# Attention followed by a feed-forward layer: the first 1427 scheduled operations follow a written list, the first loads change their order, and three early steps get more engines

## The chip, the cores and the metric

The kernel runs on one core of a Trainium2 chip. The time is the device time of one execution in microseconds; the kernel before has a median of 913.9 us over three runs (912.82 to 916.17). The engines of the core are TensorE (PE, with its weight loads as PEld), VectorE (DVE), ScalarE (ACT), GpSimd (POOL) and SyncE (SP), which here only issues DMAs. Each engine works through its own instructions strictly in the order in which the program was written.

## The reference

There are 8 batches, 8 heads, 576 positions and a head width of 64. Attention looks back over a window: heads 0 to 3 see the last 32 positions, heads 4 to 7 every fourth one of the last 128. The result goes through a feed-forward layer of 512 to 2048 to 512 whose activation is a quotient of two polynomials.

```python
scores = scale * np.matmul(q, k.transpose(0, 1, 3, 2))
scores = np.where(masks[None, :, :, :], scores, -1000000000.0)
attn = np.exp(scores - np.max(scores, axis=-1, keepdims=True))
attn = attn / (np.sum(attn, axis=-1, keepdims=True) + 1e-09)
x = np.matmul(attn, v)            # then [4608, 512]
h = x @ w_in
P = a[0] + a[1] * h + a[2] * h2 + a[3] * h3
Q = 1.0 + np.abs(b[0]) * np.abs(h) + np.abs(b[1]) * h2
return (P / (Q + 1e-06)) @ w_out
```

The weights arrive in 64-bit floats, so a 128x512 block of them is 512 KB.

## The kernel before

**Units.** Each batch's attention is cut into 6 units, 48 in all, numbered here as 0 to 47 (unit 6 is the first of batch 1). A unit loads its queries and keys (`load_qk`, 448 KB) and its values (`load_v`, 384 KB). `scores` is 48 small matmuls into a pair of PSUM banks; for batches 0 and 1 the mask is added by two or four matmuls before them. Then come `max` and `sub` on VectorE (units 6 to 11 subtract on TensorE, `sub_pe`; unit 4 does it within six exponentials, `exp_bank`), `exp` on ScalarE, `sum` and `recip` on VectorE, `norm` (GpSimd for batch 0, six ScalarE copies for batch 1), a transposition on TensorE (`transposes`, `place`) and `av`, 48 small matmuls with the values. For batch 0 the result is split from PSUM into a high and a low part (`evac_hi` on ScalarE, `evac_lo` on VectorE; `less_hi` and `copy_lo` for units 4 and 5). For later batches it goes out to DRAM and back in another layout (`put_out`, `move_out`: tiles `y` and `z` in the profile) and is split from there. From unit 8 on, the `av` of the unit two before runs together with the scores.

**Weights.** Each of the 32 weight blocks (`wi` and `wo`, 16 each) is loaded (`w_fetch`), made into 32-bit floats in three steps (`w_scale` on ScalarE, `w_low` on ScalarE or GpSimd, `w_join` on VectorE), and split into high and low (`w_hi` on ScalarE, VectorE or GpSimd; `w_lo` on VectorE or GpSimd).

**Tiles.** The feed-forward layer is 144 tiles, T0 to T143: 9 groups of 512 tokens by 16 blocks of the hidden width. A tile is `h` (12 matmuls of 128x512, high and low parts), an activation of twelve steps on ScalarE, VectorE and GpSimd, and four `out` of three matmuls each. T0 to T7 need batch 0's attention, T8 to T23 batch 1's. Two PSUM banks hold `h`; a bank comes free when the step `g2` (`a<-a,h` in the profile) has run. The steps named below: `q_lin` is `r<-a,ab_t` on ScalarE, `qq` is `a<-r,a` on VectorE or GpSimd, `g_hi` is `gh<-a`, `g_lo` is `gl<-a,gh`.

**The planner.** Every step is an operation (`op`) with the engines that may run it, its cost on each, and what it depends on. `Plan.run` goes through a modelled time, always takes the operation that can start first (with due times as ranks, lines 143 to 164), and emits its instructions; the emitted order is final on every engine. Where the model leaves TensorE idle in the first 150 us, `keep_busy` (line 217) emits filling matmuls of `ident_b`, whose result is not used. All loads are issued by SP in the emitted order, so a load that waits for a free buffer holds up the ones behind it. The early loads are put in the order of their ranks (lines 1029 to 1038).

**The start.** The masks and the six coefficients have loads of their own (`masked`, line 958, and `lc`, line 963), issued behind unit 0's queries and keys.

Of the kernel before, what the change touches and what calls it, by code (L numbers as in the profile page):

```python
# [25 lines left out]
BOTH = {"ACT": 480, "DVE": 520}  # L26
# [13 lines left out]

DEPTH, LOADS, STAGE, AHEAD, ON_PE, BY_PE = 2, 2, 6, 6, 2, 2
LEFT = S - 512
RQ, RKEY, NV = 4 * 3 * 32, 4 * 128, 3 * 2 * 2 * 64
# [18 lines left out]

class Op:
# [4 lines left out]
    def __init__(self, engs, rank, fn, deps, dma, lock):  # L68
        self.engs, self.rank, self.fn, self.dma, self.lock = engs, rank, fn, dma, lock
        self.deps = [d for d in deps if d is not None]  # L70
        self.takes, self.follows = [], []
        self.spare = None
# [9 lines left out]
class Plan:  # L82
# [7 lines left out]
    DMA_START, DMA_NS, DMA_RATE = 1000.0, 1700.0, 380.0  # L90
# [5 lines left out]
    def op(self, engs, rank, fn, *deps, dma=0, lock=False):  # L96
        o = Op(engs, rank, fn, deps, dma, lock)
        self.ops.append(o)
        return o
# [32 lines left out]
    def run(self):  # L132
        free = {}
        pipe, ports = self.DMA_START, 0.0
# [6 lines left out]
        ready = [o for o in self.ops if not left[id(o)]]  # L141
        done = 0
        while ready:
            options = []
            for o in ready:
                before = list(o.deps)
                for tag, _ in o.takes:
                    bufs, groups = self.tags[tag]
                    if len(groups) >= bufs:
                        users = groups[len(groups) - bufs]  # L150
                        if any(u.end is None for u in users):
                            break
                        before += users
                else:
                    for eng, ns in o.engs.items():
                        shared = ports if Plan.shares(o, eng) else 0.0
                        t = max([free.get(eng, 0.0), shared] + [d.after(eng) for d in before])
                        options.append((t, o, eng, ns))
            assert options, "the plan is stuck"
            first = min(x[0] for x in options)  # L160
            eng0 = min((x for x in options if x[0] == first), key=lambda x: x[1].rank)[2]
            start, o, eng, ns = min(
                (x for x in options if x[2] == eng0 and x[0] <= first + self.WINDOW), key=lambda x: (x[1].rank, x[0])
            )
            for tag, users in o.takes:
                self.tags[tag][1].append(users)
# [22 lines left out]
def tile_attention_moe(  # L189
# [27 lines left out]
    def keep_busy(n, ps):  # L217

        if n <= 0:
            return  # L220
# [881 lines left out]
```

## Time and profile before

| what | value |
|---|---|
| median of three runs | 913.9 us |
| profiled execution: span from first to last instruction | 911.9 us |
| PE, DVE, ACT, POOL busy | 887.7, 727.6, 684.8, 472.8 us |
| mean granted TensorE clock | 0.994 |
| T0's first matmul starts | 42.23 us |
| time of one `h`, and of one tile's four `out`, where nothing waits | 2.72 us each |

The profiled execution's own time is its span; the median of the runs is 2.0 us above it. A row of the stage table gives a stretch of the span, its length, then for each engine the busy time with the number of instructions, the granted TensorE clock, the DMA share and the rate. A row of a timeline gives start, duration, engine, line of the kernel, operation, tiles and in brackets the idle time before it with what ended it. L245, L248, L251, L254 and L257 are helper lines, so instructions are told apart by their tiles. In the groups, the number behind the busy time is the mean duration in ns.

### The profile page before, as it was taken

What the parts mean: (1) busy time and instruction counts of PE and PEld (TensorE: products, weight loads), DVE (VectorE), ACT (ScalarE), POOL (GpSimd) and SP (SyncE); (2) the same over time, 40 slices, a digit from 0 to 9 for tenths busy, and PEclk for the clock granted to TensorE, in tenths of its full rate; (3) what the DMA queues carried; (4) which work ended last, traced back from release to release, by engine and by line L of the source; (5) the groups of instructions that cost most, each with busy time, mean ns of one, the idle gap of its engine ahead of it and who ended that gap; (6) DMA issues with size and microseconds to landing.
All of it is one profiled execution on the core that took longest, in us unless ns stands there. A gap on an engine that the chain in (4) does not pass through costs nothing.

```text
span 911.9 us, 21320 instructions
## 1 busy us (share of the span) xinstructions
PE 887.7 (97%) x8208; PEld 714.9 (78%) x8208; DVE 727.6 (80%) x1291; ACT 684.8 (75%) x1128; POOL 472.8 (52%) x424
## 2 busy tenths in 40 slices
PE   6889999999999999999999999999999999999998
PEld 4656778877887888888888878888888888888876
DVE  4889999988998986888688886887688677566656
ACT  3888899867767777677767767777877788778774
POOL 2354666635555654555555555456455555544442
PEclk8899999999999999999999999999999999999999
DMA  9785614144643531453155441233143220001001
GB/s 339 272 281 181 241 55 147 60 127 143 192 141 113 152 93 46 131 165 112 49 173 156 135 141 65 96 104 98 47 145 108 63 70 1 0 1 47 1 1 46
DMA packets 85478, 103.46 MB, mean 113 GB/s; under 512 B 37377, under 2 KB 62849, under 8 KB 85377
## 3 DMA queue, kind: packets, MB, share of 16 engines
q1 hardware_dynamic: 85376, 102.11, 35.1%
q8 instruction: 64, 1.05, 0.5%
q14 instruction: 38, 0.30, 0.1%
HBM read 75.21 MB, written 26.87 MB: 112 GB/s over the span
## 4 chain that ended last, share of the span: by engine, by line
PE 82%; DVE 8%; DMA 4%; ACT 2%; issue 2%; POOL 1%; SPq 1%; DVEq 0%; ACTq 0%; POOLq 0%
PE out L245 39%; PE h L245 38%; PE pair L245 4%; DVE a L254 2%; DMA results<-y 1%; DVE h L254 1%; DMA z<-results 1%; ACT r L248 1%; DMA qk<-in_qk_dram 1%; DVE t L251 1%; SPq L242 1%; POOL a L257 1%; PE pair_A L245 0%; DVE a L251 0%; PE pair_B L245 0%
## 5 line engine op out<-in xcount | busy, mean ns | idle before, releaser
L245 PE MATMUL h<-xh,wi 128*128 128x512 f32 x1136 | 376.7, 393 | 5.5 <-DVE a L254 5.1
L245 PE MATMUL out<-gh,wo 128*128 128x512 f32 x1136 | 352.8, 392 | 0.0
L257 POOL TENSOR_TENSOR a<-r,a 128x512 f32<-128x512 f32 x123 | 159.2, 1294 | 259.4 <-ACT r L248 241.2
L245 PEld LDWEIGHTS h<-xh,wi 128*128 128x128 f32 x1136 | 213.3, 188 | 55.2 <-DVE a L254 9.3
L245 PEld LDWEIGHTS out<-gh,wo 128*128 128x128 f32 x1136 | 211.6, 188 | 44.9
L245 PE MATMUL out<-gl,wo 128*128 128x512 f32 x568 | 221.4, 390 | 0.6 <-POOL gl L257 0.6
L245 PE MATMUL h<-xl,wi 128*128 128x512 f32 x568 | 221.3, 390 | 0.0
L257 POOL TENSOR_TENSOR gl<-a,gh 128x512 fp32r<-128x512 f32 x137 | 182.0, 1329 | 40.9 <-ACT gh L248 31.0
L254 DVE SCALAR_TENSOR_TENSOR a<-a,r 128x512 f32<-128x512 f32 x141 | 101.4, 719 | 121.3 <-ACT r L248 119.3
L248 ACT ACTIVATE r<-a,ln_bias 128x512 f32<-128x512 f32 x141 | 101.8, 722 | 67.9 <-POOL a L257 64.5
L248 ACT ACTIVATE r<-a,ab_t 128x512 f32<-128x512 f32 x141 | 114.6, 813 | 14.6 <-DVE h L254 9.0
L245 PEld LDWEIGHTS out<-gl,wo 128*128 128x128 f32 x568 | 106.6, 188 | 23.7 <-POOL gl L257 1.2
L245 PEld LDWEIGHTS h<-xl,wi 128*128 128x128 f32 x568 | 106.7, 188 | 21.3
L248 ACT ACTIVATE a<-h 128x512 f32<-128x512 f32 x140 | 83.3, 595 | 52.4 <-PE h L245 44.2
L254 DVE SCALAR_TENSOR_TENSOR h<-t,na_t,h 128x512 f32<-128x512 f32 x142 | 107.3, 755 | 4.6
L248 ACT ACTIVATE t<-h,na_t 128x512 f32<-128x512 f32 x142 | 109.2, 769 | 1.6 <-DVE h L254 1.2
L254 DVE SCALAR_TENSOR_TENSOR h<-h,na_t,r 128x512 f32<-128x512 f32 x142 | 106.5, 750 | 4.6 <-ACT r L248 3.3
L248 ACT ACTIVATE r<-r,exp_bias 128x512 f32<-128x512 f32 x144 | 104.3, 724 | 4.7
L248 ACT ACTIVATE gh<-a 128x512 fp32r<-128x512 f32 x133 | 83.6, 628 | 27.0 <-PE out L245 24.5
L251 DVE TENSOR_TENSOR t<-t,h 128x512 f32<-128x512 f32 x142 | 95.9, 675 | 5.9 <-ACT t L248 4.9
L254 DVE SCALAR_TENSOR_TENSOR a<-a,h 128x512 f32<-128x512 f32 x140 | 96.2, 687 | 4.8
L257 POOL TENSOR_TENSOR xl<-z,xh 128x256 fp32r<-128x256 f32 (+5 forms) x52 | 39.1, 764 | 33.1 <-ACT xh L248 32.7
(123 smaller groups left out, 716.2 us busy)
## 6 DMA issues: line engine op xcount, KB each, us to landing
qk<-in_qk_dram SPq DMA_DIRECT2D x48, 448.0 KB, 5.3
v<-in_vp_dram SPq DMA_DIRECT2D x48, 384.0 KB, 3.9
out_dram<-os SPq DMA_DIRECT2D x36, 256.0 KB, 2.1
wi_raw<-in_w_in_dram SPq DMA_DIRECT2D x16, 512.0 KB, 6.2
wo_raw<-in_w_out_dram SPq DMA_DIRECT2D x16, 512.0 KB, 5.9
results<-y SPq DMA_DIRECT2D x42, 192.0 KB, 3.5
z<-results SPq DMA_DIRECT2D x168, 48.0 KB, 2.0
turned<-u SPq DMA_DIRECT2D x36, 192.0 KB, 2.2
```

The costliest lines, as they stand in the source:

```text
L242: pin(nc.sync.dma_start(dst, src))
L245: pin(nc.tensor.matmul(o, lhs, rhs, start=start, stop=stop, skip_group_check=free))
L248: pin(nc.scalar.activation(o, i, func, **kw))
L251: pin(nc.vector.tensor_tensor(o, x, y, op))
L254: pin(nc.vector.scalar_tensor_tensor(o, x, s, y, op0, op1))
L257: pin(nc.gpsimd.tensor_tensor(o, x, y, op))
```

## The change

The planner gets a list, `ORDER`, of 1427 operation numbers, some with a letter that sets the engine. Those operations are emitted first, in the list's order; the rest follow by the planner's rule as before. The list reaches to T44's `h`. On TensorE it has the same units and tiles in nearly the same order as before: T0's `h` behind unit 8's scores as before, but the scores of unit 4 ahead of unit 0's `av`, of unit 5 ahead of unit 1's, of unit 6 ahead of unit 2's and 3's, and unit 13's scores (with unit 11's `av`) ahead of T4's `h`, where they stood behind T5's. The first loads on SP go out as v0, qk0, qk1, qk2, qk3, qk4, wi1, wi2, qk5, v1, wi3, qk6, v2, v3, wi0, qk7, v4, qk8, v5, v6; before they went as qk0, coefficients, masks, v0, qk1, v1, qk2, v2, qk3, v3, qk4, v4, qk5, then four wi, qk6, qk7, and later qk8, wi, v5, v6, v7.

The masks and coefficients lie behind unit 0's values in one array (`head`), so they come with that load; a GpSimd copy keeps the masks for later batches. Three early steps may run on more engines: `norm` of batch 0 also on VectorE (the list does so for units 0 and 4), `q_lin` also on VectorE (T0 and T2) and GpSimd (seven tiles up to T35), `g_hi` also on VectorE (T34 and T35). The model's costs change, it gets the code fetches of TensorE and a limit of 8 loads under way, and a few more order constraints: T0's `h` behind the kept leftovers of batch 0, batch 2's results behind the `h` of T20, the transposed buffers in DRAM counted.

```diff
+ENGINES = {"a": "ACT", "d": "DVE", "p": "POOL", "e": "PE", "s": "SP"}
+ORDER = """
+0 3 2 6 7 18 8 9 32 10 20 21 11 48 64 34 22 12d 13 23 35 102 24 50 4 14a 36 25 37 114 38 66 26p 39 27 79 40p 1 103 28a 51 52 19 67 15 53 54 41 81 16
...
+""".split()
...
+        for item in order:
+            n, eng = (int(item[:-1]), ENGINES[item[-1]]) if item[-1] in ENGINES else (int(item), None)
+            o = self.ops[n]
+            assert id(o) in ready, "the order breaks a dependency"
+            place(*next(x for x in options(o) if eng in (None, x[2])))
+        while ready:
+            every = [x for o in ready.values() for x in options(o)]
...
         def load_v(self, pool, tag):
-            self.v = pool.tile([P, NV], F32, tag=tag, name=f"v{self.n}", bufs=LOADS if pool is att else 1)
-            load(self.v, vp[self.n])
+            if self.n:
+                self.v = pool.tile([P, NV], F32, tag=tag, name=f"v{self.n}", bufs=LOADS if pool is att else 1)
+                load(self.v, vp[self.n - 1])
+                return
+            t = pool.tile([P, NV + NMASK + 6], F32, tag=tag, name="v0", bufs=1)
+            load(t, head)
+            self.v = t[:, :NV]
+            extra["mask"] = t[:, NV : NV + NMASK].bitcast(BF16).rearrange("p (m k) -> p m k", k=64)
+            extra["coef"] = t[:, NV + NMASK :]
...
+            if self.n == 0:
+                copies.append(op({"POOL": 500}, -30, lambda e: copy(e, mask_t, extra["mask"]), lv))
+                copies.append(op({"DVE": 80}, -30, lambda e: make_coefs(), lv, consts))
+                copies.append(lv)
...
-            no = op({"ACT": 1250} if b == 1 else {"POOL": 880}, 0, lambda e: self.norm(e), rc)
+            no = op({"ACT": 1440} if b == 1 else {"POOL": 830, "DVE": 560} if start else {"POOL": 830}, 0, lambda e: self.norm(e), rc, lock=True, tail=-400 if b == 1 else 0)
...
-        def q_lin(self):
+        def q_lin(self, eng):
             tag, bufs = self.r_buf
             self.r = work.tile([P, 512], F32, tag=tag, name=f"r{self.i}", bufs=bufs)
-            act(self.r, self.a, AF.Identity, bias=ab_t[:, 0:1], scale=ab_t[:, 1:2])
+            if eng == "ACT":
+                act(self.r, self.a, AF.Identity, bias=ab_t[:, 0:1], scale=ab_t[:, 1:2])
+            else:
+                pin((nc.vector if eng == "DVE" else nc.gpsimd).tensor_scalar(self.r, self.a, ab_t[:, 1:2], ab_t[:, 0:1], ALU.mult, ALU.add))
...
-            h.follows.append(Tile.last_h)
+            h.follows += [Tile.last_h] if Tile.last_h else kept
...
-            gh = op({"ACT": 520, "POOL": 588} if self.early else {"ACT": 520}, k + LATE["gh"], lambda e: self.g_hi(e), g2)
+            gh = op({"ACT": 520, "POOL": 588, "DVE": 440} if self.early else {"ACT": 520}, k + LATE["gh"], lambda e: self.g_hi(e), g2, lock=True)
...
-    masked = op({"SP": 430}, -39.4, lambda e: load(mask_t, mask), dma=P * 768)
...
-    lc = op({"SP": 60}, -39.5, lambda e: load(coef_t, coef), dma=3000)
...
+        if i == HALF + NF - 4:
+            for o in moved[2]:
+                o.follows.append(Tile.last_h)
...
-    plan.run()
+    plan.run(order)
```

More of the change, by code (lines that the diff above doesn't have):

```diff
@@ L140, in run @@
                 after.setdefault(id(d), []).append(o)
[L141 to L164, printed above, removed]
@@ new lines, in run, with options @@
+        ready = {id(o): o for o in self.ops if not left[id(o)]}
+        def options(o):
+            before = list(o.deps)
+            for tag, _ in o.takes:
+                bufs, groups = self.tags[tag]
+                if len(groups) >= bufs:
+                    users = groups[len(groups) - bufs]
+                    if any(u.end is None for u in users):
+                        return
+                    before += users
+            queue = []
+            if o.dma:
+                parts = 0
+                for f in reversed(flying):
+                    if parts + f.parts + o.parts > self.FLYING:
+                        queue = [f.end]
+                        break
+                    parts += f.parts
+            for eng, ns in o.engs.items():
+                shared = state["ports"] if Plan.shares(o, eng) else 0.0
+                yield max([free.get(eng, 0.0), shared] + queue + [d.after(eng) for d in before]), o, eng, ns
@@ L165, in run, with place @@
+        def place(start, o, eng, ns):
             for tag, users in o.takes:
@@ L741, in plan_weights @@
             steps = [op({"DVE": 335}, 0, lambda e: w_copy(key), f)]
-        hi = op({"ACT": 550, "DVE": 460, "POOL": 680}, 0, lambda e: w_hi(key, e), steps[-1], lock=True)
-        lo = op({"DVE": 625, "POOL": 1350}, 0, lambda e: w_lo(key, e), hi, lock=True)
+        hi = op({"ACT": 521, "DVE": 440, "POOL": 690}, 0, lambda e: w_hi(key, e), steps[-1], lock=True)
+        lo = op({"DVE": 605, "POOL": 1350}, 0, lambda e: w_lo(key, e), hi, lock=True)
         plan.takes(steps[0], "stage", STAGE, [lo])
@@ L1035, in tile_attention_moe @@
     loads = sorted(early, key=lambda o: o.rank)
+    order = ORDER if wide else []
+    listed = {int(x.strip("adpes")) for x in order}
+    loads = [o for o in loads if plan.ops.index(o) not in listed]
     for o, before in zip(loads[1:], loads):
         o.follows.append(before)
-    plan.run()
+        o.loose = before
+    plan.run(order)
 _OUT = (DM, NC, 512)
```

205 lines of the change are left out of this document (142 added, 63 removed).

## The prediction

> **What bounds the kernel now.** I read the busy time by stages first, cut where T0's first `h` starts (42.23), where T12's starts (132.40), where the new list ends (T44's `h`, 321.90) and ahead of the tail.
>
> ```profile
> span 911.9 us, 21320 instructions
> 0.00:42.23 42.23, 31.43 (x847) 21.88 (x847) 25.32 (x62) 23.30 (x70) 12.15 (x27) 0.88 0.82 298
> 42.23:132.40 90.17, 81.97 (x812) 60.95 (x811) 84.92 (x143) 78.23 (x146) 50.67 (x45) 1.00 0.58 205
> 132.40:321.90 189.50, 188.79 (x1909) 153.03 (x1908) 173.10 (x315) 145.34 (x235) 105.21 (x92) 1.00 0.44 132
> 321.90:895.00 573.10, 572.23 (x4594) 468.36 (x4588) 434.11 (x760) 432.04 (x673) 302.37 (x261) 1.00 0.27 81
> ```
>
> The columns are stretch, length, then PE, PEld, DVE, ACT, POOL busy. From 132 us to 895 us TensorE idles 1.6 us of 762.6: there nothing can be won, only lost. All that can be won lies ahead of 132 us. In the second stretch TensorE idles 8.2 us, and the busy part holds fillers:
>
> ```profile
> L245 PE MATMUL out<-ident_b,zeros_b 128*128 128x512 bf16 x23 | 5.7, 381 | 0.0
> L245 PE MATMUL out<-ident_b 128*128 128x512 bf16 x13 | 3.5, 379 | 0.0
> PE h L245 <- DVE a L254: 5.1, 4, 1.6
> PE pair_B L245 <- issue: 3.9, 2, 3.4
> ```
>
> That is 9.2 us of filler, so 17.4 us of the 90.2 do no work, while VectorE is busy 84.9 (94%). TensorE's longest waits (second pair of rows: the waits of the first 135 us) are for `a<-a,h`, VectorE's step that frees an `h` bank. VectorE is the limit of this stretch, with 5.3 us of slack. The first stretch is a chain of loads, scores, VectorE and TensorE; its timeline on TensorE:
>
> ```profile
> 6.13 0.72 PE L245 MATMUL pair_A<-qk 64*32 64x64 f32 x48
> 8.99 0.72 PE L245 MATMUL pair<-qk 64*32 64x64 f32 x48 [1.64 <-DMA qk<-in_qk_dram]
> 11.08 0.97 PE L245 MATMUL pair_A<-qk 64*32 64x64 f32 x48 [0.88 <-DMA qk<-in_qk_dram]
> ...
> 21.16 0.61 PE L245 MATMUL pair_B<-pT,v 64*64 64x32 f32 x18 [3.39 <-issue]
> ...
> 22.85 0.97 PE L245 MATMUL pair<-qk 64*32 64x64 f32 x48
> ...
> 29.15 0.72 PE L245 MATMUL pair<-qk 64*32 64x64 f32 x48
> ...
> 37.67 0.90 PE L245 MATMUL pair_A<-pT,v 64*64 64x32 f32 x48 [0.41 <-DMA v<-in_vp_dram]
> ...
> 42.23 0.53 PE L245 MATMUL h<-xh,wi 128*128 128x512 f32 x1
> ```
>
> The `qk` rows at 6.13, 8.99, 11.08, 22.85 and 29.15 are the scores of units 0, 1, 2, 5 and 6. Units 1 and 2 wait for their loads; 832 KB of keys and values lie between them and take 2.09 us, 408 GB/s. Inside unit 1's `av` TensorE stands 3.39 us with "issue" as the reason, no engine and no load: I read it as instructions that had not arrived. Unit 5's `av` at 37.67 waits for v5, which SP issued late, behind a load for unit 8 that needs the buffer unit 6 reads until 29.87:
>
> ```profile
> 30.02 0.40 SPq L242 DMA_DIRECT2D qk<-in_qk_dram  x1
> 30.48 0.42 SPq L242 DMA_DIRECT2D wi_raw<-in_w_in_dram  x1
> 30.95 3.25 SPq L242 DMA_DIRECT2D v<-in_vp_dram  x3
> ```
>
> ```profile
> qk<-in_qk_dram SPq DMA_DIRECT2D x48, 448.0 KB, 5.3
> v<-in_vp_dram SPq DMA_DIRECT2D x48, 384.0 KB, 3.9
> ```
>
> **The first stretch: 7 us earlier.** The masks and coefficients move behind v0 and two small loads go. By bytes nothing changes up to unit 1's keys (v0, masks, qk0, qk1 are the same 1.4 MB), so I take 0 for the first scores and up to 1 us either way. Moving the keys ahead of the values takes 384 KB from before unit 2's keys and 384 KB more from before each later unit's: at 408 GB/s 0.96 us for unit 2, 1.9 for unit 3, 2.9 for unit 4. Against that v1 to v4 come later. Summed by bytes, v1 has some 3.2 MB after qk1 ahead of or in it: about 17 us, v2 about 20.5, v4 about 25; their `av` stand behind the scores of units 5, 6 and 7 in the list, at 16 to 26 us below, so this hides, and costs what it is late if those scores come sooner.
>
> Then VectorE paces. The list puts ahead of unit 3's subtraction four maxima, four subtractions, three sums, three reciprocal pairs and unit 0's `norm`. The rows are of the first 150 us:
>
> ```profile
> L345 DVE TENSOR_REDUCE mx<-pair 128x6 f32<-128x384 f32 x11 | 6.0, 547 | 1.3 <-PE pair L245 1.2
> L251 DVE TENSOR_TENSOR p<-pair,mx 128x384 f32<-128x384 f32 x5 | 2.8, 551 | 0.0
> L381 DVE TENSOR_REDUCE sm<-p 128x6 f32<-128x384 f32 x13 | 7.1, 547 | 0.8 <-ACT p L248 0.8
> L385 DVE RECIPROCAL sm<-sm 128x6 f32<-128x6 f32 x14 | 2.7, 192 | 0.5
> L384 DVE TENSOR_SCALAR sm<-sm 128x6 f32<-128x6 f32 x14 | 2.2, 158 | 0.4
> L257 POOL TENSOR_TENSOR p<-p,sm 128x384 f32<-128x384 f32 x8 | 7.9, 982 | 17.8 <-DVE sm L385 16.0 <-ACT wi_f L704 1.8
> ```
>
> The trace has no `norm` on VectorE; it is a two-input step on 128x384, nearest the subtraction, so 0.55, bounded by 0 and by GpSimd's 0.98. With eleven steps of 0.55, three pairs of 0.35 and `norm`, 7.7 us follow the first scores' end at 6.9; with 1.5 us for the waits on exponentials and on unit 1's keys, unit 3 is subtracted at 16, and unit 5's scores can start, against 22.85. A stall for instructions like the 3.39 us one can fall here, as the loads are packed just as tightly: 16 to 19. Eight more VectorE steps (4.2 us, unit 4's `norm` among them) lead to unit 6's scores at 20.2 to 22, against 29.15.
>
> From there to T0's `h` took 13.1 us before. Now two more `av` (0.9 us each) stand in between, and v5 is issued behind unit 8's keys again, but 8 us earlier, and lands ahead of its `av`. VectorE's listed work in between is 15.3 us by such rows, 14.7 before. So 13 to 15.3 us, and T0's `h` at 33.2 to 37.3: I take 35.2, **7.0 us earlier**. Ends: 9 (no stall), and 0 if the stalls add up.
>
> [...]
>
> **The second stretch: 3 us less.** From T0 to T12 the list gives VectorE, against before, +5 `g_lo`, +2 `q_lin`, +1 `qq`, +2 `w_lo`, +1 of the 0.75 us steps, and takes away 5 `evac_lo`, 5 `w_hi`, one `w_join`, one `place` and a unit's `sum` and `recip`. By the rows of the first 150 us:
>
> ```profile
> L251 DVE TENSOR_TENSOR a<-r,a 128x512 f32<-128x512 f32 x12 | 10.1, 839 | 0.8 <-ACT r L248 0.4
> L254 DVE SCALAR_TENSOR_TENSOR a<-a,r 128x512 f32<-128x512 f32 x14 | 12.0, 859 | 0.0
> L260 DVE CAST wo<-wo_f 128x512 fp32r<-128x512 f32 x4 | 1.7, 427 | 0.1
> L248 ACT ACTIVATE r<-a,ab_t 128x512 f32<-128x512 f32 x15 | 12.2, 813 | 2.2 <-DVE a L254 2.0
> ```
>
> Eight two-input steps (`g_lo`, `qq`, `w_lo`) at 0.85, `q_lin` at 0.43 and the 0.75: 6.8+0.9+0.75 = 8.5 more. Less: five `evac_lo` of one or two pieces at 0.86 (4.3), five `w_hi` at 0.43 (2.1), `w_join` 0.86, `place` 0.55, `sum` and `recip` 0.9: 8.7. The difference is nothing, so the limit stays at 85 us. (`q_lin` on VectorE isn't in the trace; it has one input like the cast, 0.43; upper bound 0.84 as for two inputs, +0.8 in all.) ScalarE loses four `q_lin` (3.2 us). What is left is VectorE's slack of 5.3 us, and two places of it are named:
>
> ```profile
> 55.99 0.56 DVE L251 TENSOR_TENSOR xl<-z,xh 128x384 fp32r<-128x384 f32 x1 [1.31 <-ACT xh L248]
> 102.84 1.68 PE L245 MATMUL out<-ident_b,zeros_b 128*128 128x512 bf16 x7
> 106.15 0.50 PE L245 MATMUL h<-xh,wi 128*128 128x512 f32 x1 [1.62 <-DVE a L254]
> ```
>
> At 55.99 VectorE stands 1.31 us on a result of batch 1 that comes through DRAM, with T0's `g2` queued behind it, and T1's `h` behind that; in the list GpSimd takes all six of these steps. At 102.8 to 106.2 TensorE loses 3.3 us ahead of T8, batch 1's first tile; unit 11's `av` now stands two tiles earlier. I take 1.3 and half of the 3.3, **3 us**. Ends: 5.3 gained (no slack left), 4 lost, which is VectorE's 85 us 5% longer where it meets GpSimd.
>
> **The third stretch: 2 us more.** Here the list moves GpSimd's work to VectorE. Counted from T12 to T44: `qq` on VectorE 9 to 18, `g_lo` 4 to 6, `g_hi` 0 to 2, `w_join` 9 to 12, `w_lo` 1 to 3, one more unit's sum, reciprocal and split, less three activation steps, two evacuations and one `w_hi`.
>
> ```profile
> L251 DVE TENSOR_TENSOR a<-r,a 128x512 f32<-128x512 f32 x10 | 6.9, 693 | 2.3 <-ACT r L248 1.3 <-POOL wo L257 0.5
> L254 DVE SCALAR_TENSOR_TENSOR wo_f<-wo_f,wo_raw 128x512 int32<-128x512 int32 x8 | 7.2, 896 | 0.0
> L254 DVE SCALAR_TENSOR_TENSOR a<-a,r 128x512 f32<-128x512 f32 x32 | 22.5, 702 | 1.1 <-ACT r L248 1.1
> ```
>
> At 0.69 for `qq` and `g_lo`, 0.43 for `g_hi`, 0.90 for the weights' steps, 1.8 for the unit's and 0.7 for most of those taken away, 6.2+1.4+0.9+2.7+1.8+1.8 less 4.1 is 10.7 us more on VectorE, beside which stand the 16.4 us that it idles there: 183.8 of 189.5. The cover is 5.7 us, and TensorE has but two `h` banks. At 97% I expect some of it to show: **2 us**. Ends: 0, and 6.
>
> Behind the list nothing of a tile's work changes, and the tail (from 895) keeps its steps: 0. A wait that the list adds, batch 2's results behind T20's `h`, holds only SP's later loads. The sum is 911.9 - 7 - 3 + 2 = 903.9 for the execution; the median stands 2.0 above its execution before, so **906 us**.
>
> **The rivals.** *VectorE becomes the bound of the third stretch* (slower). Steps with two inputs cost 0.86 in the first 150 us where they meet GpSimd's, and 0.70 later (the `a<-a,r` rows). If the third stretch pays the early price, its 32 such steps and 18 `qq` cost 0.15 each, 7.5 us more, and half of the present idle time (8 us) is waits that can't be filled: 183.8+7.5+8 = 199.3, 10 us over TensorE's 189.5. It decides once VectorE needs more than 189.5 us there. With the second stretch at +4 and the first at -7: 913.9 + 7 = 921; with the second at 0, 917. For it: VectorE at 97%. Against: GpSimd runs ten `qq` and three `g_lo` fewer there, so it collides less. Chance 0.13, at 918.
>
> [...]
>
> *The start stays where it is.* Code stalls and SP's order (v5 again behind a load that must wait) hold T0's `h` at 40 or later; then -2 in the first stretch, -2 in the second, +2: about 912. For it: the 3.39 us row and DMA at its full 408 GB/s. Against: the rows at 22.85 and 29.15 show no wait for a load, and 17 loads of the list are out before SP meets one that must wait for an engine. Chance 0.24.
>
> *All slack goes*: -9, -5.3 and 0 give 899.5. For it: every idle row above has a name in the list. Against: it needs three ends at once. Chance 0.18.
>
> *The list isn't used* (it is only for 64-bit weights) is excluded by the row below: 512 KB for 128x512 values is 8 bytes each.
>
> ```profile
> wi_raw<-in_w_in_dram SPq DMA_DIRECT2D x16, 512.0 KB, 6.2
> ```
>
> **How the numbers follow.** My forecast has 0.45, with its own range of 902 to 910. About 0.5%, 4.6 us, is what this kernel's measurement can tell from no change. Faster by more: all of the third rival, nine tenths of the forecast and a little of the second, 0.62; slower by more: two thirds of the first rival and some of what nobody named, 0.12; the same 0.26. The range of 899 to 915 takes in the forecast, the second and third rivals' middles, and leaves out most of the first rival.
>
> **What would show it.** T0's `h` between 33 and 37 us, unit 6's scores at 20 to 22; T12's `h` near 122; T44's near 314, with TensorE's idle and filler between them small. It is wrong if T0's `h` starts at 40 or later, or if from T12 to T44 VectorE is above 99% and TensorE idles more than 5 us.

## The result, and the profile after

The changed kernel takes 923.7 us (median of four runs, 921.5 to 924.1); the kernel before, measured beside it, 913.4 (912.0 to 916.2). The ratio is 1.0095, with an interval of 1.007 to 1.0121: about 1% slower, where the forecast was 906 with a range of 899 to 915. First the stage table of the changed kernel, cut at the times of the prediction's table (stretch, length, PE, PEld, DVE, ACT and POOL busy, granted clock, DMA share, GB/s):

```profile
span 922.3 us, 21264 instructions
0.00:42.23 42.23, 34.18 (x856) 24.93 (x856) 24.98 (x66) 22.19 (x67) 15.50 (x29) 0.84 0.82 300
42.23:132.40 90.17, 79.61 (x797) 61.95 (x796) 82.53 (x140) 76.99 (x145) 46.97 (x45) 0.98 0.59 194
132.40:321.90 189.50, 183.61 (x1781) 146.47 (x1780) 178.52 (x319) 139.70 (x226) 97.23 (x86) 0.99 0.45 135
321.90:905.00 583.10, 579.50 (x4693) 468.98 (x4692) 439.59 (x766) 435.45 (x679) 303.41 (x262) 1.00 0.25 80
```

From 132 to 322 TensorE, busy 188.8 us before, is busy 183.6; VectorE goes from 173.1 to 178.5. More telling is when the same tile starts. The first `h` of T0, T12, T24, T34, T35, T44 and T48 and the last `out` on TensorE's timeline of the changed kernel, with the largest wait between them:

```profile
39.52 0.54 PE L335 MATMUL h<-xh,wi 128*128 128x512 f32 x1
126.15 0.39 PE L335 MATMUL h<-xh,wi 128*128 128x512 f32 x1
200.97 0.50 PE L335 MATMUL h<-xh,wi 128*128 128x512 f32 x1 [0.43 <-DVE a L344]
262.34 0.50 PE L335 MATMUL h<-xh,wi 128*128 128x512 f32 x1
267.44 0.50 PE L335 MATMUL out<-gh,wo 128*128 128x512 f32 x1 [2.04 <-DVE os L341]
271.88 0.40 PE L335 MATMUL h<-xh,wi 128*128 128x512 f32 x1
324.48 0.50 PE L335 MATMUL h<-xh,wi 128*128 128x512 f32 x1
349.18 0.39 PE L335 MATMUL h<-xh,wi 128*128 128x512 f32 x1
917.22 0.39 PE L335 MATMUL out<-gl,wo 128*128 128x512 f32 x1
```

The same tiles from T12 on in the kernel before:

```profile
132.45 0.39 PE L245 MATMUL h<-xh,wi 128*128 128x512 f32 x1
202.13 0.50 PE L245 MATMUL h<-xh,wi 128*128 128x512 f32 x1
263.29 0.39 PE L245 MATMUL h<-xh,wi 128*128 128x512 f32 x1
269.95 0.50 PE L245 MATMUL h<-xh,wi 128*128 128x512 f32 x1
321.94 0.50 PE L245 MATMUL h<-xh,wi 128*128 128x512 f32 x1
343.83 0.39 PE L245 MATMUL h<-xh,wi 128*128 128x512 f32 x1
907.89 0.39 PE L245 MATMUL out<-gl,wo 128*128 128x512 f32 x1
```

| from | to | change, us | forecast |
|---|---|---|---|
| start | T0 | -2.7 | -7 |
| T0 | T12 | -3.6 | -3 |
| T12 | T24 | +5.1 | +2, for T12 to T44 |
| T24 | T34 | +0.2 | |
| T34 | T35 | +2.9 | |
| T35 | T44 | +0.6 | |
| T44 | T48 | +2.8 | 0 |
| T48 | last `out` | +4.0 | 0 |
| last `out` | end | +1.0 | 0 |

So the list does bring T12 6.3 us forward, and everything behind it gives 16.7 us back, at four places with different causes, which the experiments take one by one. The 1.0 us behind TensorE's last `out` has no known cause.

Two of the rows hide an exchange of work. By T34 the list has one more unit's scores and `av` done; the kernel before does them between T34 and T35, where they take 1.4 us of TensorE. By T48 the changed kernel has done half a tile's `out` more, again 1.4 us. On equal work T24 to T34 gains 1.2 us, T34 to T35 loses 4.2, T44 to T48 1.5, and the rest behind T48 5.3.

The stretches are compared within one profiled execution each. Where the instructions are the same they repeat: T12 to T24 takes 74.8 to 74.9 us in the changed kernel and in four others with its order there. The start does not repeat: in the twelve profiled kernels with the list's start T0's `h` lies between 38.8 and 42.4 us, so the -2.7 is uncertain by more than its own size.

### The profile page after: what moved, and what is told of

It is laid out like the page before. It is cut to its first block, busy times and chain, and to the rows that moved or that the text cites. A ratio compares the mean times of both kernels' runs of the same rounds, so it can differ in the third digit from the quotient of the medians.

```text
span 922.3 us, 21264 instructions
## 1 busy us (share of the span) xinstructions
PE 889.5 (96%) x8175; PEld 712.4 (77%) x8175; DVE 735.2 (80%) x1302; ACT 679.6 (74%) x1121; POOL 465.1 (50%) x421
## 4 chain that ended last, share of the span: by engine, by line
PE 70%; DVE 16%; ACT 4%; issue 4%; DMA 3%; POOL 2%; SPq 1%; DVEq 0%; ACTq 0%; POOLq 0%
PE h L335 32%; PE out L335 31%; PE pair L335 5%; DVE a L344 4%; DVE h L344 4%; ACT r L338 2%; DMA wo_raw<-in_w_out_dram 1%; DVE t L341 1%; SPq L332 1%; PE pair_A L335 1%; DMA z<-results 1%; DVE a L341 1%; DVE wi_f L344 1%; POOL a L347 1%; DVE wo_f L344 1%
## 5 line engine op out<-in xcount | busy, mean ns | idle before, releaser
L347 POOL TENSOR_TENSOR a<-r,a 128x512 f32<-128x512 f32 x113 | 146.2, 1294 | 275.2 <-ACT r L338 245.8
L347 POOL TENSOR_TENSOR gl<-a,gh 128x512 fp32r<-128x512 f32 x130 | 171.7, 1320 | 38.4 <-ACT gh L338 24.7
L338 ACT ACTIVATE r<-a,ab_t 128x512 f32<-128x512 f32 x132 | 107.5, 814 | 32.3 <-DVE h L344 21.5
L335 PEld LDWEIGHTS out<-gl,wo 128*128 128x128 f32 x568 | 107.0, 188 | 25.6 <-DVE gl L341 2.0
L347 POOL TENSOR_TENSOR xl<-z,xh 128x256 fp32r<-128x256 f32 (+5 forms) x58 | 48.1, 845 | 30.1 <-ACT xh L338 29.6
```

The source lines that it names most:

```text
L335: pin(nc.tensor.matmul(o, lhs, rhs, start=start, stop=stop, skip_group_check=free))
L338: pin(nc.scalar.activation(o, i, func, **kw))
L347: pin(nc.gpsimd.tensor_tensor(o, x, y, op))
```

## The experiments

Times are medians with the ratio to the kernel before, measured beside each (913.4 to 915.3).

**Is it the order at all?** Two kernels use the changed program with another list. `e3_oldorder` lists all operations in the order and on the engines of the kernel before (a few stand a little later, where a buffer that the changed planner counts forces it):

```diff
 ORDER = """
-0 3 2 6 7 18 8 9 32 10 20 21 11 48 64 34 22 12d 13 23 35 102 24 50 4 14a 36 25 37 114 38 66 26p 39 27 79 40p 1 103 28a 51 52 19 67 15 53 54 41 81 16
+0p 2s 3s 1p 18s 19s 32s 33s 48s 49s 4p 5d 64s 6e 65s 79s 96s 102s 7d 114s 20e 126s 8d 288s 9a 299s 10d 11d 34e 21d 12p 22d 23a 13e 35d 24d
...
```

> All operations in the order and on the engines of the kernel before, in the changed program: masks and coefficients behind v0, the identity's other buffer. It measures the change without its order. If order and engines are the whole of it, 912 to 915 as before, with T0's h at 41 to 43; if the merged load counts, T0's h moves by more than 1 us and the end with it.

Measured: 914.6, ratio 1.0001 (0.9985 to 1.0018). T0's `h` starts at 44.0, later than the 41 to 43 that were expected, but the end did not move with it. Every tile from T12 on keeps nearly its distance to the kernel before (2.6 us at T12 and T24, 1.4 to 1.7 from T34 on). The merged first load and the other edits of the program are worth nothing that can be measured; within the 1.6 us that the interval leaves, order and engines are the whole change.

`e4_nolist` has an empty list:

```diff
-    order = ORDER if wide else []
+    order = []
```

> The changed program with an empty list: its planner orders every operation with its new costs. Theory A (the new costs order the rest worse): TensorE behind T44 loses 6 us or more against before here too, as in the changed kernel (T44's h to the end 593 us against 586). Rival B (the loss behind T44 comes from the list's state): behind T44 the pace is that of before, 586 us. Ahead of T44 no theory gives a number; the list is good for what this kernel's T44 comes later than 324.5.

Measured: 956.9, ratio 1.0452 (1.0407 to 1.0497). From T44's `h` to TensorE's last `out` it takes 591 us, against 593 in the changed kernel and 586 before. That is 5 us lost, a little less than the 6 of theory A and far from rival B. All of it falls behind T48 (569.4 us, 564.1 before); T44 to T48 takes 21.7 us, 21.9 before. So the planner with its new costs loses behind T48 without any list, and far more ahead of it: T44 comes at 360.2.

**The loss behind the list.** `e1_oldrest` keeps the list and appends the remaining 2323 operations in the order of the kernel before:

```diff
-1864 615 1865 1853 1866 616 617 1839 1867 1879 621 1868 608 1877 1878 1869 620 1894 622 1870 656 1880 628 606 623 629 618 607d
+1877a 1878a 1869d 620s 1894e 622d 1870a 656s 1880p 628d 606a 623s 629d 618s 607d 1881d 1882d 1883a 630d 1884a 1871p 631a 1885d 1854e 1895a
...
```

> The 1427 listed operations as in the changed kernel; every later operation stands in the order, and on the engines, that the kernel before gave it. Theory A (the 7 to 8 us lost behind T44 come from the order of the rest, which the new costs of the scores, exponentials and transfers planned anew): T44's h stays at 324.5 and TensorE then keeps the pace of before, so the end comes 6 to 8 us earlier than in the changed kernel, 916 to 918 us. Rival B (the loss behind T44 is owed by the state in which the list leaves the engines): no change, 922 to 925.

Measured: 920.7, ratio 1.0076 (1.0057 to 1.0095). The interval still touches that of the changed kernel, but the profile is clear: from T48 on each tile stands 6.3 to 5.7 us behind the kernel before, without further loss, where the changed kernel goes on to lose 4.0. From T44 to T48 it still loses 2.3. So both theories hold in part: the newly planned rest costs 4 us of the profile (2 to 3 by the ratios and the medians), and about 2 us right behind T44 are owed by the list. The longest of TensorE's waits from 349 to 900 us in the changed kernel (total, times, longest):

```profile
PE h L335 <- DVE a L344: 2.0, 5, 0.9
```

With the old rest there is no such wait. The five waits are only half of the 4.0 us; for the rest TensorE is busy longer in this stretch (565.7 us, 563.2 before) and does not wait. What the new costs changed in the order to bring either was not taken apart.

**Is the lead at T12 a loan?** Ahead of T12's `h`, by the two orders, the kernel before has done four weight joins on VectorE (wi10, wi12, wi13, wi14) that the list puts off; of the others the list has done one more. `e2_splice12` follows the list up to T12's `h` and then the order of before:

```diff
-1284d 1274a 1286 1258 390 226a 406 1287 1275p 1288 1298 213 1299 1290 206a 407 1289 1291 205 391 1300p 392 1292a 1302d 1293d 1301 393 1303 396 1304
+1273d 1285d 1282a 1260e 1284d 1274a 1286d 1258e 390d 226a 406d 1287a 1275p 1288a 1298e 396s 236a 235a 213d 246s 214a 248a 215d 260p 247a
...
```

> The list only up to T12's h, and from there the order and the engines of the kernel before. Theory A (the third stretch loses by the list's own choice of engines, VectorE being full from T12 to T24): T12's h stays at 126 and the lead of 6.3 us is kept but for the 3 us of VectorE work that the list has put off until behind T12 by the rows' prices: T44's h at 316 to 319, the end 3 to 6 us ahead of before, 907 to 910. Rival (the lead at T12 is all a loan: work put off, which any order has to pay): T44's h at 321 to 323 and 912 to 915.

Measured: 919.6, ratio 1.0051 (1.003 to 1.0071), worse than either theory. Both were too simple: in the order of before all put-off steps stand at the very front of what is left, so they come in one lump. Two rows of VectorE's timeline behind T12's `h`, the first weight step of the lump and its longest idle time:

```profile
131.11 1.12 DVE L454 SCALAR_TENSOR_TENSOR wi_f<-wi_f,wi_raw 128x512 int32<-128x512 int32 x1
...
141.21 0.64 DVE L628 STREAM_TRANSPOSE u<-p 128x192 f32<-128x192 f32 x2 [3.20 <-POOL p L457]
```

T12's `h` starts at 129.4, T13's at 146.3, 16.9 us later in place of 5.4, and 54 of the filling matmuls, 11.8 us long, cover the hole on TensorE. From T13 to the end the distance to the kernel before goes only from 8.4 to 7.4. The order of before loses nothing behind T13, and a splice is no clean test of a debt.

`e10_oldstart` is the better one: the order of before up to T0's `h`, then what is left of the list, then the order of before.

```diff
-0 3 2 6 7 18 8 9 32 10 20 21 11 48 64 34 22 12d 13 23 35 102 24 50 4 14a 36 25 37 114 38 66 26p 39 27 79 40p 1 103 28a 51 52 19 67 15 53 54 41 81 16
+0p 2s 3s 1p 18s 19s 32s 33s 48s 49s 4p 5d 64s 6e 65s 79s 96s 102s 7d 114s 20e 126s 8d 288s 9a 299s 10d 11d 34e 21d 12p 22d 23a 13e 35d 24d
...
```

> The order of the kernel before up to T0's h, then what is left of the list in the list's order, and behind it the order of before (as in e1_oldrest). Ahead of T0's h VectorE has then done the low part of the weights of wi4 and the joins of wi5 and wi6, 2.6 us, that the list puts off. Theory A (the list's lead at T0's h is work put off): T0's h at 43 to 44.5 as in e3_oldorder, and yet T12's h at 126 to 128.5, as in the kernels with the list's start; the end within 2 us of e1_oldrest, 919 to 922. Rival B (an early T0 is a real gain): T12's h later by what T0's h is later, 129 to 131, and the end 923 to 925.

Measured: 920.8, ratio 1.0077 (1.0059 to 1.0094), as `e1_oldrest` and as theory A said; rival B wanted 923 to 925. So the list's early T0 is worth nothing at the end. How much of it is gone by T12 stays open. Against `e1_oldrest` T0 is 2.9 us later (43.75 and 40.85) and T12 1.1 (128.76 and 127.69), which would be two thirds; but these are single executions, and T12 alone lies between 124.8 and 129.4 in the kernels with the list's start.

**From T12 to T24: VectorE full, or something else?** `e5_pool` moves twenty steps between T12 and T44 from VectorE to GpSimd and keeps every position in the order (three of them: T11's `g_lo`, T15's `qq`, wi12's low part):

```diff
-1293d
+1293p
...
-1356d
+1356p
...
-239d
+239p
```

> The whole order of the changed kernel, but twenty steps from T12 to T44 that the list puts on VectorE go to GpSimd, as before: ten qq, five g_lo, two g_hi and three w_lo. By the rows some 13 us of VectorE's 178.5 in that stretch go. Theory A (VectorE bounds the third stretch): T12's h stays at 126, and T44's h comes 3 to 6 us earlier than in the changed kernel, at 318 to 321; the end 918 to 920. Rival B (what bounds there is the length of a tile's chain through the engines, and GpSimd's 1.3 us for a step against VectorE's 0.7 make it longer): T44's h at 324 or later, the end 923 or more.

Measured: 922.3, ratio 1.0088 (1.0065 to 1.0112). In groups of VectorE's instructions, first the changed kernel from 126 to 201 us, with its stage row:

```profile
126.00:201.00 75.00, 71.59 (x579) 56.31 (x577) 74.05 (x118) 62.22 (x101) 40.45 (x34) 1.00 0.30 92
L344 DVE SCALAR_TENSOR_TENSOR a<-a,r 128x512 f32<-128x512 f32 x12 | 10.4, 866 | 0.2 <-issue 0.2
L341 DVE TENSOR_TENSOR a<-r,a 128x512 f32<-128x512 f32 x11 | 9.1, 823 | 0.1
```

then the kernel before, from 132 to 202:

```profile
L254 DVE SCALAR_TENSOR_TENSOR a<-a,r 128x512 f32<-128x512 f32 x12 | 8.1, 678 | 0.0
L251 DVE TENSOR_TENSOR a<-r,a 128x512 f32<-128x512 f32 x9 | 6.2, 693 | 2.3 <-ACT r L248 1.3 <-POOL wo L257 0.5
```

and `e5_pool`:

```profile
126.00:201.00 75.00, 73.34 (x589) 58.32 (x588) 69.41 (x115) 63.95 (x103) 51.77 (x45) 1.00 0.31 97
L454 DVE SCALAR_TENSOR_TENSOR a<-a,r 128x512 f32<-128x512 f32 x12 | 11.3, 946 | 4.2 <-ACT r L448 4.2
```

In the changed kernel VectorE is busy 98.7% of this stretch, idles nowhere, and pays 0.87 for the step that cost 0.68: the rival of the prediction, by its rows. But with VectorE at 92.5% and 4.2 us of idle time in front of `a<-a,r` alone, T12 to T24 still takes 72.8 us: 2.0 of the 5.1 come back, 3.1 stay, and a single step has become dearer still (0.95). Full occupancy can't be what holds these 3.1. Behind T24 `e5_pool` loses 1.2 of the 2.0 again (T34 to T35 costs 3.6 us more than before, not 2.9), and its T12 came 1.0 later, so T44 at 324.6 is a miss for theory A.

`e11_less` leaves out the two steps that make and join the low words of wi10, wi12, wi13 and wi14, the put-off ones; `e12_mended_less` does the same in the mended kernel described below.

```diff
+    PUT_OFF = {("wi", n) for n in (10, 12, 13, 14)}
...
     def w_join(key):
+        if key in PUT_OFF:
+            return
```

> The changed kernel in its own order, with the decoding of four weights cut short: for wi10, wi12, wi13 and wi14 the two steps that make and join the low words are left out (four VectorE steps of 1.0 us, two each on ScalarE and GpSimd), so these weights keep only their upper words. These are the four joins that the kernel before had done ahead of T12's h and the list puts behind it. Theory A (the 5 us lost from T12 to T24 are these put-off steps and the steps moved to VectorE): T12's h stays at 126 to 127.5, and T12 to T24 takes 74.8 less 3 to 4, 70.8 to 71.8 us (69.7 before). Rival B (something else bounds there, the chain through GpSimd or the small stops): 73.5 or more.

> The same eight steps left out of the kernel e9_mended, where ten steps stand on GpSimd and VectorE is busy 69.4 of 75 us from 126 to 201. There T12 to T24 takes 72.85 us. Theory A (the 3.1 us that are left against before are the put-off steps): 69.7 to 70.7. Rival B (with VectorE relieved, what is left is the longer chain of the steps on GpSimd, and the put-off steps hide): 72 or more.

Measured: 921.5, ratio 1.0077 (1.0059 to 1.0095), T12 to T24 in 73.4 us (74.8 with the steps); and 911.1, ratio 0.9973 (0.9957 to 0.9988), 73.1 us (72.85 with them). Theory A falls: 4 us of VectorE's work gone bring 1.5 us where VectorE is full and nothing where it isn't. The joins put off ahead of T12 are at most a part of what costs behind it. They are not all that was put off: by the two orders the list also leaves until behind T12 the subtractions for the low parts of wi10 to wi14 (it has done wo9's instead), four of which GpSimd had done ahead of T12, and eleven steps of ScalarE for the weights (it has done two others). These were not taken out by themselves.

What does cost shows in the mended kernel on the timelines of VectorE and GpSimd:

```profile
170.52 1.43 DVE L454 SCALAR_TENSOR_TENSOR a<-a,r 128x512 f32<-128x512 f32 x1 [0.46 <-ACT r L448]
...
173.88 1.62 DVE L451 TENSOR_TENSOR a<-r,a 128x512 f32<-128x512 f32 x1
```

```profile
170.10 1.30 POOL L457 TENSOR_TENSOR wi<-wi_f,wi 128x512 fp32r<-128x512 f32 x1
...
173.66 1.29 POOL L457 TENSOR_TENSOR wo<-wo_f,wo 128x512 fp32r<-128x512 f32 x1
```

Both VectorE steps begin just after GpSimd started the subtraction for a weight's low part, and end 0.55 us after it has ended: they stand through it. TensorE then stands for an `h` bank:

```profile
173.72 0.50 PE L445 MATMUL h<-xh,wi 128*128 128x512 f32 x1 [0.65 <-DVE a L454]
```

The pattern holds for all `a<-a,r` and `a<-r,a` of this stretch (126 to 201 us). Eight of the twenty begin while a step of GpSimd runs; each ends 0.53 to 0.55 us after that step, and they take 0.69 to 1.62 us. The other twelve take 0.65 to 0.69, also where GpSimd starts a step during them. In the changed kernel eight of 22 begin so, and take 0.78 to 1.72; in the kernel before, from 132 to 202 us, two of 21, which fell so late in GpSimd's step that they cost nothing (0.68 and 0.69). `e13_one_input` writes zeros for the low parts of thirteen such weights with a one-input step of GpSimd:

```diff
     def w_lo(key, eng):
+        if eng == "POOL" and key in ONE_INPUT:
+            pin(nc.gpsimd.tensor_scalar(wt[key][:, 1], wf.pop(key), 0.0, None, ALU.mult))
+            return
         either(eng, wt[key][:, 1], wf.pop(key), wt[key][:, 0], ALU.subtract)
```

> e9_mended with the low part of thirteen weights (wo8 to wo14 and wi10 to wi15, less wo10's order, all between T11 and T24) written as zeros by a step of GpSimd with one input in place of the subtraction with two: the low parts of these weights are left out of the result. From T12 to T24 e9_mended takes 72.85 us against 69.68 before, though VectorE idles 5.6 us of 75; there VectorE's a<-a,r takes 1.44 us at 172 and a<-r,a 1.62 us at 175, in place of 0.69, while GpSimd runs such a subtraction, and TensorE stops 0.3 to 0.8 us for an h bank behind them. Theory A (the remaining 3.1 us are VectorE's steps shut out by GpSimd's): the mean of a<-a,r there falls from 0.95 to 0.75 or less and T12 to T24 takes 69.7 to 70.7 us. Rival B (the order of the tiles' steps itself is what costs): 72 or more.

```profile
L454 DVE SCALAR_TENSOR_TENSOR a<-a,r 128x512 f32<-128x512 f32 x13 | 10.4, 796 | 4.6 <-ACT r L448 4.6
L951 POOL TENSOR_SCALAR wo<-wo_f 128x512 fp32r<-128x512 f32 x6 | 10.3, 1709 | 0.0
```

Measured: 910.0, ratio 0.9952 (0.9933 to 0.997); T12 to T24 takes 71.6 us. The mean of `a<-a,r` falls from 0.95 to 0.80, and 1.3 of the 3.1 us go, between the two theories. GpSimd's step did not become shorter (1.71 us, against 1.52 for the subtraction), but VectorE no longer waits for it: the four steps that begin inside one take 0.67 to 0.77 us. (It also needs no high part of the weight, but that wait was only 1.1 us in all in the mended kernel.) So shutting out by the weights' subtractions is shown as a cause, for something like 1.3 us; 1.9 us against the kernel before have no proven cause. Three steps still stand through other work of GpSimd (0.90 to 1.65 us), and the put-off steps named above are a rival that no run here tests.

`e14_low_on_vector` lets VectorE do twelve of these subtractions instead:

```diff
-239p
+239d
...
-281p
+281d
```

> e9_mended with twelve of these subtractions on VectorE, which does the whole work: 12 x 0.69 us = 8.3 us on an engine that idles 5.6 of 75. Theory A (a GpSimd step with two inputs costs VectorE more than it takes off it when it falls on a tile's steps): no loss, T12 to T24 at 72 to 73 us or less, and the end within 1 us of e9_mended. Rival B (VectorE's occupancy decides): VectorE above 98%, T12 to T24 at 74 to 76, the end 2 us later than e9_mended.

Measured: 914.3, ratio 0.9992 (0.9978 to 1.0006); T12 to T24 takes 75.5 us, as rival B said, though VectorE is busy only 72.1 of 75 us (96%). Between these two engines moving the steps one way brought 2.0 us in this stretch (`e5_pool`), and moving them the other way cost 2.6; neither reached the 69.7 of before.

**T34 to T35: a reload behind the wrong buffer.** The reload of parked sum 1 goes through SP and GpSimd of the changed kernel like this:

```profile
260.00 0.36 SPq L332 DMA_DIRECT2D out_dram<-os  x1
263.80 0.32 SPq L332 DMA_DIRECT2D os<-part  x1
```

```profile
262.74 1.03 POOL L347 TENSOR_TENSOR xl<-z,xh 128x384 fp32r<-128x384 f32 x1
```

SP stands from 260.4 to 263.80, until GpSimd's split has read the staging buffer (`z` of unit 18) that the reload gets. VectorE's addition to it, and TensorE behind the `out` bank that it frees, wait with it: the 2.04 us at 267.44. Right behind this stop TensorE runs 3.41 us at half its clock (from 267.86). What that costs can be read from two kernels with the same order here: in `e1_oldrest`, with the half clock, T34 to T35 takes 9.57 us, in `e10_oldstart`, without it, 8.17. `e6_reload` issues that load behind the reload of sum 2 (the turning of unit 19's result then stands three places later):

```diff
-538 525 1672 1685 1686
+538d 525s 1672s 1669s 1685a 1686a
...
-547 1690a 1691p 1677 541 1669 1702
+1690a 1691p 1677s 547d 541d 1702d
```

> The changed kernel's order with one load moved: the reload of the parked sum 1 (os1) stands right behind that of sum 2, not behind T31's third store. In the changed kernel it got the buffer that GpSimd's split of unit 18 reads until 263.77, was issued at 263.80, and TensorE stood 2.04 us for it at 265.4 and ran 3.41 us at half clock from 267.86. Theory A (that wait is the 4 us jump between T34 and T35): T35's h 2.5 to 3.7 us earlier against T34's, and the end as much, 920 to 921. Rival B (VectorE has no slack there, so the wait moves to an h bank): less than 1 us, 922.5 to 924.

Measured: 921.7, ratio 1.0081 (1.0054 to 1.0108). T34 to T35 takes 7.25 us in place of 9.54 (6.66 before), and the tiles up to T48 keep the 2.3 us: a little less than the 2.5 to 3.7 of theory A. Only 0.7 of the 2.3 is a shorter wait, since 1.4 us of it stay, with VectorE's turning now behind that split; the rest, 1.6 us, is about what the half clock costs, which is gone here. At the end the gain is not clear of the noise.

`e7_combo` joins the old rest, the twenty steps on GpSimd and the moved reload:

> The list, with its twenty steps on GpSimd and the reload moved as in the two kernels of this call, and behind the list the order and engines of the kernel before, which took 2.6 us off the changed kernel. If all three act on their own the sum is 923 - 2.6 - 4.5 - 3 = 913, the time of the kernel before; if the steps on GpSimd and the reload share one slack, 915 to 917; if GpSimd's longer chain costs what VectorE gains, 920.

Measured: 915.9, ratio 1.0006 (0.9989 to 1.0024): between the first two sums, no slower than before. T12 to T24 still takes 72.85 us; what is left of the loss behind T24 sits at T34 (1.49 us of waiting) and at T45. There, as in the changed kernel, VectorE does a split in two pieces ahead of T44's steps, while GpSimd idles 4.89 us before its next step:

```profile
326.19 1.97 DVE L341 TENSOR_TENSOR xl<-z,xh 128x160 fp32r<-128x160 f32 x2
```

```profile
332.32 1.30 POOL L347 TENSOR_TENSOR a<-r,a 128x512 f32<-128x512 f32 x1 [4.89 <-ACT r L338]
```

**A version that beats both.** `e9_mended` gives these splits of three units back to GpSimd, keeps only ten of the twenty moved steps there, and puts the addition to reloaded sum 1 ahead of unit 19's turning:

```diff
-569d
+569p
...
-588d
+588p
...
-607d
+607p
```

> As e7_combo, with three changes: of the steps put on GpSimd only those up to T23 stay there (ten: four g_lo, three qq, three w_lo), the splits of units 14 to 16 of the later batches (U3.2 to U3.4) go from VectorE to GpSimd too, and T31's fourth part and its addition to the reloaded sum 1 stand ahead of unit 19's turning. In e7_combo VectorE spent 2 us on such a split ahead of T45, where TensorE waited 1.77 us for an h bank and then ran 3.41 us at half clock, and 1.49 us ahead of T32's out. Theory A (these two places are the rest of the loss behind T34): the 1.8 us from T44 to T45 and 1.5 us from T34 to T35 go, and the end comes 3 to 5 us ahead of e7_combo, 911 to 913, at or just under the kernel before. Rival B (GpSimd is late with the splits, so the next batch's x or VectorE's h waits): 915 or more.

```profile
132.40:321.90 189.50, 187.82 (x1900) 150.70 (x1899) 175.17 (x317) 144.61 (x234) 115.64 (x104) 1.00 0.47 142
```

Measured: 911.7, ratio 0.9975 (0.9961 to 0.999), just faster than the kernel before and 1.2% faster than the changed one. T34 to T35 takes 5.6 us, T44 to T48 22.7 (24.7 in the changed kernel, 25.6 in `e7_combo`), and TensorE no longer waits at either place. The three edits were made together, so their shares are not told apart. T12 to T24, at 72.85, is what it still loses.

**The start.** `e8_fillers` counts a filler at 120 ns instead of 240, so four more fillers stand ahead of unit 1's mask, four ahead of unit 5's, and some behind (the expectation puts the second four too early):

```diff
-BUSY_UNTIL, BUSY_LESS, BUSY_NS, BUSY_FIRST, KEEP = 150000.0, 250.0, 240.0, 14, 0
+BUSY_UNTIL, BUSY_LESS, BUSY_NS, BUSY_FIRST, KEEP = 150000.0, 250.0, 120.0, 14, 0
```

> The changed kernel with fillers counted at 120 ns each in place of 240, so more of them stand where the plan sees TensorE wait: four more ahead of unit 1's mask copies, four ahead of unit 4's, ten more ahead of T0 to T2. Theory A (the stalls without a releaser in the first stretch are instructions that arrive late, and belong to a place in TensorE's instruction stream, not to a piece of work): the stalls stand at the same instruction number (the matmuls number 223 and 351 of the trace), which is eight matmuls earlier in the work: at the end of unit 3's scores and 17 matmuls into unit 5's in place of 1 into unit 4's and 25 into unit 5's. Rival B (they belong to a load or to an engine that the profile doesn't show): they stay ahead of the same matmul of unit 4 and of unit 5. The half clock ahead of T0's h, 13.65 us, shrinks if waits ahead of 13 us bring it, T0's h then comes 1 to 2 us earlier; it stays if the stalls bring it, and T0's h stays at 39.5 within 1 us. The end within 2 us of the changed kernel either way.

TensorE in the changed kernel, then in this one:

```profile
12.90 0.24 PE L335 MATMUL pair_A<-qk 64*32 64x64 f32 x1
14.69 0.71 PE L335 MATMUL pair_A<-qk 64*32 64x64 f32 x47 [1.54 <-issue]
16.16 1.51 PE L335 MATMUL pair_B<-pT,v 64*64 64x32 f32 x48
...
18.75 0.65 PE L335 MATMUL pair<-qk 64*32 64x64 f32 x25
20.88 0.65 PE L335 MATMUL pair<-qk 64*32 64x64 f32 x23 [1.48 <-issue]
...
24.92 0.85 PE L335 MATMUL pair<-qk 64*32 64x64 f32 x48
```

```profile
12.16 0.71 PE L335 MATMUL pair<-qk 64*32 64x64 f32 x47
15.10 0.27 PE L335 MATMUL pair<-qk 64*32 64x64 f32 x1 [2.23 <-issue]
```

The first stall falls after 223 matmuls of the trace in both; four of them are fillers here that the changed kernel lacks, and so the work it cuts into moves by four, from unit 4's scores (one done of 48) to the end of unit 3's (47 done). A later one, of 0.83 us at 34.63 in the changed kernel and 1.87 at 35.65 here, stands after 731 matmuls in both. So the stalls belong to a place in TensorE's instruction stream, as theory A said; that they are instructions that arrive late stays the author's reading and is not shown. The old order says it more strongly: `e3_oldorder`, with other work at these places, stalls after 223 and 351 matmuls too (1.59 and 3.26 us), and the kernel before after 223 and 350 (0.47 and the 3.39 of the prediction). In the changed kernel's trace 128 matmuls and 128 weight loads lie between the first two places, 256 instructions. The stall after 351 is not seen in this kernel. The half clock doesn't shrink (two stretches of 6.83 us), and T0's `h` at 41.5 lies within the scatter of the start. The time, 929.0 (ratio 1.0164, 1.0137 to 1.0191), is above what was expected. The rest behind the list is planned anew here, and from T64 to T100, which the list doesn't touch, TensorE idles 4.2 us, against 0.8 in the changed kernel.

## Why the prediction was wrong

Two terms failed most. The third stretch was to cost +2 because VectorE's 183.8 us would just fit beside TensorE; it cost +8.8. Behind the list the forecast was 0; it was +7.8, of which 1.0 lies behind the last `out`.

**The first stretch, -7: mis-sized, measured -2.7.** Up to unit 5 the times came out, but in part by luck: unit 3's subtraction starts at 16.3 (forecast 16), unit 5's scores at 18.75 (16 to 19). VectorE had the steps ahead of this subtraction done at 14.6, earlier than forecast, and then waited for TensorE's transposition, which stood behind the first stall:

```profile
16.32 0.56 DVE L341 TENSOR_TENSOR p<-pair,mx 128x384 f32<-128x384 f32 x1 [1.74 <-PE t L498]
```

From unit 6's scores to T0's `h` it took 14.6 us (13 to 15.3). The step that failed is the one between them, the eight VectorE steps of 4.2 us that were to bring unit 6's scores at 20.2 to 22 (from the forecast's own 19 it should have said 23.2): they start at 24.92. The forecast allowed for one stall; there were two, 1.54 and 1.48 us, and between and behind them TensorE was granted half its clock, so an `av` took 1.51 us in place of 0.90:

```profile
15.27:25.51 10.24, 8.68 (x214) 6.81 (x208) 5.46 (x15) 6.26 (x21) 2.91 (x8) 0.50 0.67 260
```

With TensorE busy 8.68 of these 10.24 us it was TensorE, not VectorE, that paced. The list did not bring the stalls: in the order of before they stand after the same matmuls (see `e8_fillers`). The second error is that an early T0 was taken as a gain in full; `e10_oldstart` shows nothing of it at the end.

**The second stretch, -3: right in size, at -3.6, but not in its working.** T12's `h` at 126.15 is later than the 122 named only by what the first stretch lacked, and the two named waits are gone (TensorE waits for no bank ahead of T1, and 0.48 us ahead of T8). But VectorE's work, which was to stay at 85 us and be the limit, is 77.9 of 86.6 us. The forecast put the early price of 0.85 on its two-input steps here; the list made them cheaper, the kernel before first, from 42.23 to 132.45 us, then the changed one, from 39.52 to 126.15:

```profile
L254 DVE SCALAR_TENSOR_TENSOR a<-a,r 128x512 f32<-128x512 f32 x11 | 10.0, 908 | 0.0
L344 DVE SCALAR_TENSOR_TENSOR a<-a,r 128x512 f32<-128x512 f32 x11 | 7.9, 721 | 0.1
```

At the same time new waits came, for other steps of VectorE and for a stall of 2.16 us: TensorE idles 10.6 us in place of 8.2, with 2.0 us of filler in place of 9.2. That these add up to -3.6 is partly luck.

**The third stretch, +2: wrong, at +8.8.** The counts of steps were right within one or two (19 `qq`, 6 `g_lo`, 12 joins), the prices were not: 0.77 for `a<-a,r` and 0.92 for `qq`, where the forecast took 0.70 and 0.69. VectorE needs 187.2 us from T12 to T44, not 183.8, and the cover does not hold. Three things were missed. From T12 to T24 VectorE reached 98.7% by paying the price of the first 150 us, as the rival said (0.87 and 0.82 us for steps of 0.68 and 0.69); of the 5.1 us lost there, giving steps back to GpSimd returned 2.0. A further 1.3 is GpSimd's subtractions for weights shutting VectorE out at the moment when TensorE needs a bank, which a sum of busy times can't show; 1.9 stay open. And between T34 and T35 a reload got a buffer still being read, so SP stood: 2.0 us of waiting and a half clock behind it. The prediction looked at what SP's later loads wait for, but only for batch 2's results.

**Behind the list, 0: wrong.** That "nothing of a tile's work changes" was true and beside the point: the order does. The diff shows new costs for the scores, exponentials and transfers, and the rest is planned with them; with the order of before in its place these 4.0 us are gone. Of the 2.8 from T44 to T48 half is `out` done early; the other half goes with a wait ahead of T45, which is gone in `e9_mended`, where GpSimd does the splits (two other edits go with them).

**The signs and the rivals.** Of the signs of being wrong neither came in full: T0's `h` started at 39.5, not 40, and from T12 to T44 TensorE idled 6.0 us but VectorE was at 94%. "VectorE becomes the bound of the third stretch", at 917 to 921 and a chance of 0.13, was nearest, but it holds only from T12 to T24 and for some 2 us; its "10 us over TensorE's 189.5" happened for more reasons than its own. "The start stays where it is" nearly came true in the first stretch (T0 at 39.5, with stalls as its reason) and not in the sum. The range ended at 915 since every loss was sought in VectorE's busy time, and the part behind the list was given no loss at all.

## What to carry to other kernels

Read a lead in a stage together with what each engine has done by then: compare the sets of finished operations of both orders at the same tile, TensorE's too, and count a lead only when it is still there at the end. When two engines shut each other out, a stretch's busy share says little, and a step's price from one order doesn't carry over to another (0.91 became 0.72 in one stretch and 0.68 became 0.87 in the next); look for single instructions that take twice their usual time and for what the other engine runs beside them. From 126 to 201 us of the changed kernel the eight `a<-a,r` and `a<-r,a` of VectorE that began during a step of GpSimd took 0.78 to 1.72 us, the other fourteen 0.66 to 0.69; and the seven two-input steps of GpSimd on 128x512 that began during one of these took 1.38 to 1.73 us, seven of its twelve others 1.26 to 1.30. And in a written order each buffer's last reader matters as much as its engine: a few edits at named waits (a reload, three splits, ten steps, one addition) took `e1_oldrest` from 920.7 to 911.7 us.

## What the hardware showed that was not expected

The same instructions at the start do not take the same time. In the changed kernel and in `e1_oldrest` TensorE's first 700 instructions are the same, and the second stall takes 1.48 us in the one (above) and 3.17 in the other:

```profile
21.11 0.65 PE L445 MATMUL pair<-qk 64*32 64x64 f32 x23 [3.17 <-issue]
```

The scatter of T0's `h` over the kernels with the list's start, 38.8 to 42.4 us, is more than the whole measured gain of that stretch.

Whether a stop of TensorE costs its clock is not decided by its length. In `e7_combo` a stop of 1.77 us ahead of T45 is followed by 3.41 us at half clock; in `e10_oldstart` one of 2.29 us at 270.17 is followed by none:

```profile
331.07:334.48 3.41, 3.41 (x10) 2.64 (x9) 2.84 (x6) 2.06 (x4) 2.32 (x3) 0.50 0.23 68
```

```profile
270.30:273.70 3.40, 3.40 (x15) 2.79 (x16) 3.15 (x5) 1.05 (x2) 1.35 (x2) 1.00 0.99 288
```

What does decide it no run here shows.

A GpSimd step with one input and one operation (multiply by zero, `e13_one_input`) took 1.62 to 1.71 us for 128x512 in the mean of its groups, longer than the two-input subtraction it replaced (1.47 to 1.52), while its copies of the same shape, also with one input but two operations, took 0.74 to 0.77 in the same stretch. Yet VectorE's steps that began inside the slow one were not held (0.67 to 0.77 us), while one that began inside such a copy ended 0.54 us after it, as behind the two-input steps, and took 0.99.
